# A gated attention and state-space kernel: skip term by a diagonal, tail tables in the lag stream, gates by a selection, and a refitted order

## The chip, the cores and the metric

One core of a Trainium2 chip runs the whole kernel. The metric is the device time of one execution in microseconds (us). The kernel before took a median of 389.49 us in three runs (388.06 to 393.62). One launch computes everything; inputs and output lie in DRAM.

The granted clock is the share of full speed that the profile reports. A run is called slow when it is more than 1.5% above the fastest of the same kernel in that series.

## The reference, cut to what matters

Two branches over the same 2048 x 512 input `x`, mixed by a gate per token:

```python
g = sigmoid((x * gate_w).sum(-1, keepdims=True))     # one gate per token
a = attention(x, wq, wk, wv, wo, beta)               # 32 heads, 4 segments of 512 tokens, with a memory
b = state_space(x, A, B, C, log_dt, Dskip)           # long convolution K * x, plus x * Dskip
return g * a + (1 - g) * b
```

The kernel computes the convolution as a transform over 4096 points cut in two: a first level, then 16 "lags" (pairs of frequencies), each with a product of spectra, then an output stage. In the profile the kernel falls into four stretches: until the last product that builds the table of powers ("tables end"); from there to the last exponential of the attention scores; the lags that remain until the last of them is stored to DRAM ("last V store"); and the end, with sixteen final DVE instructions and the output stores. Attention and lags share the engines wherever their order allows it.

The profiles name the engines so: PE is TensorE, which does the matmuls and leaves their results in PSUM; DVE is VectorE, ACT is ScalarE, POOL is GpSimd; SP is SyncE, whose queue issues the DMA transfers. An evacuation is a copy of results out of PSUM.

## The kernel before

Instructions are not issued in the order in which they are written. A small list scheduler in the kernel takes, for each engine, the ready operation with the lowest `key`; estimated costs decide when it is ready. The keys of attention, tables and lags come from eight tuned numbers. Which operation may hold a PSUM bank pair follows from the same order.

```python
KEYS = (11.26, 11.5, 60.5, 67.9, 3.16, 10.8, 43.9, 16.9)
PEN, MASKD = 6.53, 25
...
o.key = (self.key if key is None else key)
...
GA, TA0, TT0, TT = KEYS[:4]                  # attention group gi of (s, hg): key TA0 + GA * (8*s + 2*hg + gi)
tail(TT0 + 4 * TT + KEYS[6])                 # lag t: key k0 + 4 + KEYS[4] * t
```

The gates stand as one column per block of 128 tokens; the final stage needs them with 16 tokens a partition. They go through DRAM to change shape:

```python
if s == 3:
    S.dma(lambda: bass.AP(gbuf, 0, [[1, 128], [128, 16]]), lambda: ap(gcolT, n=16), 8192, r=gcolP, w=[dG], slow=True)
    S.dma(lambda: ap(g4T, n=16), lambda: bass.AP(gbuf, 0, [[16, 128], [1, 16]]), 8192, r=[dG], w=[g4T])
    op("DVE", 0.2, lambda e: e.tensor_scalar(ap(omg4T, n=16), ap(g4T, n=16), -1.0, 1.0, ALU.mult, ALU.add), ...)   # L899
```

The skip term `x * Dskip` is formed on DVE from a second load of `x`, and added to the result in PSUM by a product with the identity:

```python
for gq in range(4):
    S.dma(... xj <- x, 524288 ...)
    op("DVE", c_f1(2048), lambda e, u=u: e.tensor_tensor(u, u, dskbT (fp32, broadcast), ALU.mult), key=k0 + 45)    # L1266
    ...
    for bl in range(4):
        mm(e, ap(P, n=512), ap(ident, n=128), ap(u, bl * 512, n=512), True, False)
        for c in range(2):
            i = mm(e, ap(P, n=512), ap(G2T, c * 128, n=128), ap(V2, ...), False, c == 1)
        op("DVE", c_dps(512), ... e.scalar_tensor_tensor(aj, P, omg4T, aj, ALU.mult, ALU.add) ...)                  # L1281, the last sixteen
```

A lag reads its own slice of one table (`Dt`) and slices of two 1 MB tables (`M2`, `N1`) that are loaded once. The spectral product needs the negated imaginary part of K, which DVE makes for each lag.

The softmax here doesn't subtract the row's maximum and nothing guards it: scores larger than these inputs give would overflow.

## Time and profile before

| | before, first profile | before, profiled again |
|---|---|---|
| time, us | 398.8 | 386.63 |
| span, us; mean granted clock | 397.0; .886 | 384.8; .92 |
| tables end | 256.6 | 246.8 |
| last score exponential ends | 301.5 | 287.4 |
| last V store begins | 370.4 | 356.3 |
| first of the last sixteen DVE instructions | 380.8 | 367.0 |

The first profile is what I had for the prediction. The second was taken with the experiments. A line of stretches gives, after the span, the busy time of PE, weight loads, DVE, ACT and POOL, with the number of instructions, then the granted clock, the share of DMA and its GB/s. These are the four stretches of the second profile:

```profile
0.00:246.80 246.80, 216.72 (x2653) 98.99 (x2654) 215.42 (x419) 215.87 (x291) 3.15 (x9) 0.94 0.21 58
246.80:287.40 40.60, 29.81 (x506) 12.73 (x505) 26.00 (x57) 29.76 (x35) 0.00 (x0) 0.77 0.63 203
287.40:356.30 68.90, 67.53 (x414) 26.07 (x412) 58.14 (x87) 40.68 (x43) 0.00 (x0) 0.99 0.71 205
356.30:384.80 28.50, 13.87 (x52) 5.37 (x49) 10.99 (x16) 1.37 (x2) 0.00 (x0) 0.75 0.54 189
```

### The profile page before, as it was taken

To read this page: it belongs to the slowest core of one execution; us is meant where nothing else is said; L and a number is where in the kernel's file an instruction comes from. 1 tells how busy PE (TensorE), PEld (TensorE's weight loads), DVE (VectorE), ACT (ScalarE), POOL (GpSimd) and SP (SyncE) were. 2 spreads that over 40 slices of the span, in tenths; PEclk is the share of its full clock that TensorE was granted. 3 is DMA by queue.
4 is the path that set the end of the run, shared out by engine and by line. 5 is a ranking of instruction groups with operands and counts; after the bars stand their busy time and mean duration, and the time that the engine had idled before them with its cause. 6 is when DMAs were issued, how large, how long until landed. Compare 5 with 4: busy or idle time off the path is not lost.

```text
span 397.0 us, 8521 instructions
## 1 busy us (share of the span) xinstructions
PE 334.2 (84%) x3578; PEld 146.6 (37%) x3619; DVE 311.6 (78%) x579; ACT 288.6 (73%) x369; POOL 3.2 (1%) x9
## 2 busy tenths in 40 slices
PE   5876598899798799989999999919798999999283
PEld 3333143333344333534545434405234433333131
DVE  4889979977659887989898699827676899888164
ACT  4999979968768968968898999918775587555300
POOL 1000000000000000000000000000000000000000
PEclk9996579958769959999999999976958999999879
DMA  8910003000334430021000101123992967876573
GB/s 201 302 38 2 2 0 107 2 0 0 107 107 117 134 132 2 2 37 41 14 2 3 33 3 41 17 90 141 294 296 46 325 192 182 227 211 185 183 264 159
DMA packets 41238, 42.10 MB, mean 106 GB/s; under 512 B 18928, under 2 KB 34544, under 8 KB 40816
## 3 DMA queue, kind: packets, MB, share of 16 engines
q1 hardware_dynamic: 41200, 41.56, 35.4%
q8 instruction: 28, 0.46, 0.5%
q14 instruction: 10, 0.08, 0.1%
HBM read 28.30 MB, written 13.25 MB: 105 GB/s over the span
## 4 chain that ended last, share of the span: by engine, by line
PE 50%; DVE 22%; DMA 12%; ACT 10%; issue 3%; SPq 1%; DVEq 0%; ACTq 0%
PE psum L709 48%; ACT sb L1015 5%; DVE sb L257 4%; DMA sb<-in_A_x_dram 4%; DVE sb L1138 3%; DMA scr_gbuf<-sb 3%; DVE sb L1135 3%; DVE sb L1133 3%; ACT sb L256 2%; DVE sb L1281 2%; PE psum L1045 2%; DMA sb<-in_A_wq_dram 1%; DMA sb<-scr_V 1%; SPq L252 1%; DMA scr_abuf<-sb 1%
## 5 line engine op out<-in xcount | busy, mean ns | idle before, releaser
L709 PE MATMUL psum<-sb 128*32 128x20 bf16 (+12 forms) x3362 | 317.0, 283 | 50.2 <-DVE sb L1019 8.4
L709 PEld LDWEIGHTS psum<-sb 128*128 128x128 bf16 (+4 forms) x3403 | 131.0, 98 | 232.3 <-issue 106.2
L1015 ACT ACTIVATE sb<-psum 128x1024 bf16<-128x1024 f32 x160 | 156.8, 1027 | 31.6 <-PE psum L709 30.9
L256 ACT ACTIVATE sb<-psum 128x1024 bf16<-128x1024 f32 (+4 forms) x103 | 81.7, 808 | 42.3 <-PE psum L709 36.6
L257 DVE CAST sb<-psum 128x512 bf16<-128x512 f32 (+2 forms) x60 | 50.6, 845 | 32.2 <-PE psum L709 31.6
L1138 DVE TENSOR_TENSOR sb<-sb 128x512 bf16<-128x512 bf16 (+3 forms) x52 | 34.7, 667 | 1.4
L1133 DVE TENSOR_TENSOR sb<-sb 128x512 bf16<-128x512 bf16 (+3 forms) x52 | 34.6, 665 | 0.8
L1135 DVE TENSOR_TENSOR sb<-sb 128x512 bf16<-128x512 bf16 (+3 forms) x52 | 34.2, 657 | 0.0
L259 ACT ACTIVATE sb<-psum,sb 128x512 bf16<-128x512 f32 x30 | 20.7, 690 | 4.9 <-PE psum L709 3.5
L1281 DVE SCALAR_TENSOR_TENSOR sb<-psum,sb 128x512 bf16<-128x512 f32 x16 | 10.9, 745 | 12.6 <-DMA sb<-scr_abuf 12.5
L260 DVE TENSOR_SCALAR sb<-psum,sb 128x512 bf16<-128x512 f32 x18 | 13.4, 746 | 2.5 <-PE psum L709 1.8
L1045 PE MATMUL psum<-sb 128*128 128x128 bf16 x128 | 11.5, 242 | 0.8 <-ACT sb L259 0.5
L1019 DVE TENSOR_TENSOR sb<-sb 128x512 bf16<-128x512 bf16 (+1 forms) x21 | 10.3, 501 | 2.1 <-ACT sb L1015 2.1
L1235 DVE TENSOR_TENSOR sb<-sb 128x1024 bf16<-128x1024 bf16 x16 | 11.1, 693 | 0.6
L1239 DVE TENSOR_TENSOR sb<-sb 128x1024 bf16<-128x1024 bf16 x16 | 11.1, 692 | 0.6
L1053 DVE TENSOR_TENSOR sb<-psum,sb 128x512 bf16<-128x512 bf16 x16 | 11.1, 691 | 0.5
L256 ACT ACTIVATE sb<-sb 128x512 bf16<-128x512 f32 (+2 forms) x21 | 11.3, 578 | 0.3
L1237 DVE TENSOR_TENSOR sb<-sb 128x1024 bf16<-128x1024 bf16 x16 | 10.9, 684 | 0.0
L1045 PEld LDWEIGHTS psum<-sb 128*128 128x128 bf16 x128 | 9.0, 109 | 3.7 <-issue 1.3
L1072 DVE TENSOR_TENSOR sb<-psum,sb 128x256 bf16<-128x256 f32 x24 | 9.0, 418 | 0.4
L925 DVE TENSOR_SCALAR sb<-psum 128x512 bf16<-128x512 f32 x12 | 8.2, 686 | 1.3 <-ACT sb L924 1.2
L1266 DVE TENSOR_TENSOR sb<-sb 128x2048 bf16<-128x2048 bf16 x4 | 9.1, 2284 | 0.0
(64 smaller groups left out, 129.6 us busy)
## 6 DMA issues: line engine op xcount, KB each, us to landing
sb<-in_A_x_dram SPq DMA_DIRECT2D x12, 512.0 KB, 5.5
sb<-c_D SPq DMA_DIRECT2D x16, 320.0 KB, 7.0
scr_Z<-sb SPq DMA_DIRECT2D x16, 256.0 KB, 2.6
sb<-scr_Z SPq DMA_DIRECT2D x4, 1024.0 KB, 11.4
scr_V<-sb SPq DMA_DIRECT2D x16, 256.0 KB, 5.4
sb<-scr_V SPq DMA_DIRECT2D x16, 256.0 KB
scr_abuf<-sb SPq DMA_DIRECT2D x16, 128.0 KB, 3.0
sb<-scr_abuf SPq DMA_DIRECT2D x4, 512.0 KB, 5.5
```

What stands on the lines that cost most here:

```text
L256: fa = lambda e: e.activation(dst(), src(), ACT.Copy)
L257: fd = lambda e: e.tensor_copy(dst(), src())
L259: fa = lambda e: e.activation(dst(), src(), ACT.Copy, scale=scale())
L260: fd = lambda e: e.tensor_scalar(dst(), src(), scale(), None, ALU.mult)
L709: mm = lambda e, o_, l, r_, st, sp, **kw: e.matmul(o_, lhsT=l, rhs=r_, start=st, stop=sp, skip_group_check=True, **kw)
L1015: op("ACT", c_act(1024), lambda e, P=P, pT=pT, sj=sj: e.activation(ap(pT, sj * 1024, n=1024), ap(P, n=1024), ACT.Exp, scale=0.25), r=[P], ...
L1045: i = e.transpose(ap(P, tb * 256 + gi * 128, n=128), ap(ra[gi], tb * 128, n=128), ap(ident, n=128))
L1053: op("DVE", c_dps(512), lambda e: e.tensor_tensor(ap(o1, dims=[[128, 4], [16, 8], [1, 16]]), ap(P, dims=[[256, 4], [32, 8], [1, 16]]), ap( ...
L1133: op("DVE", c_tt(256 * n), lambda e: e.tensor_tensor(run(tile, ne, dst, 1), run(tile, ne, src, sstep), pwv(0), ALU.mult), r=rd + [pw], w=w ...
L1135: op("DVE", c_tt(256 * n), lambda e: e.tensor_tensor(run(t2, n, 0, 1), run(tile, ne, src, sstep), pwv(1), ALU.mult), r=rd + [pw], w=[t2])
L1138: op("DVE", c_tt(256 * n), lambda e: e.tensor_tensor(D_(), D_(), ap(t2, n * 128, [[-n * 128, 2], [2 * n, 64], [1, 2 * n]]), ALU.add), r=[t ...
L1281: op("DVE", c_dps(512), lambda e, P=P, aj=aj, bl=bl, b4=b4: e.scalar_tensor_tensor(ap(aj, bl * 512, n=512), ap(P, n=512), ap(omg4T, b4, n= ...
```

## The change

Its intent is to take work off DVE and off the DRAM path, and then to mix attention and lags anew. In five parts, as the prediction letters them:

- (a) The gates are laid out by a product with a 0/1 selection on PE instead of the trip through DRAM.
- (b) The skip term becomes four matmuls of 128 columns with a diagonal of `Dskip`, for which `x` transposed is kept on chip. The load of `x` and DVE's four products go.
- (c) The two big tables become slices of the lag's own table. The sign moves into a subtraction, so the negation of K goes.
- (d) The relu of K may run on ACT; two more attention groups are masked on DVE (`MASKD`).
- (e) New keys, single shifts of keys (`ORDER`) and new cost estimates, so another order of everything.

A filler that would keep PE busy in its waits is in the code too, but `FILL = 0` leaves it out: PE stays idle in its waits. The core of the diff, cut:

```diff
-PEN = 6.53
-MASKD = 25
-KEYS = (11.26, 11.5, 60.5, 67.9, 3.16, 10.8, 43.9, 16.9)
+FILL, FILL0, FILLM = 0, 15.0, 0.1
+PEN = 4.0
+MASKD = 23
+KEYS = (12, 2.52, 50.32, 60, 5.74, 12.49, 34.52, 14.72)
+ORDER = {'proj2.1': -6.4, 'oph3.2': 4.1, 'oph2.3': -11.9, 'grp1.3.0': -9.7, 'oph1.3': 2.3, 'K6': 2.9, 'grp2.2.0': -23.2}
...
-        o.key = (self.key if key is None else key)
+        o.key = (self.key if key is None else key) + ORDER.get(self.tag, 0.0)
...
-    S.dma(lambda: bass.AP(gbuf, 0, [[1, 128], [128, 16]]), lambda: ap(gcolT, n=16), 8192, r=gcolP, w=[dG], slow=True)
-    S.dma(lambda: ap(g4T, n=16), lambda: bass.AP(gbuf, 0, [[16, 128], [1, 16]]), 8192, r=[dG], w=[g4T])
+    op("DVE", 0.3, ... gselT = gcolT (broadcast) * selT, 128 elements ...)
+    op("PE", 0.3, lambda e: mm(e, ap(P4, n=16), ap(gselT, n=128), ap(selT, 8, n=16), True, True), ...)
...
-    op("DVE", c_dps(512), ... rk = max(P, 0) ...)
+    op("ANY", 0.0, None, r=[P], w=[rk], alts={"ACT": ... ACT.Relu ..., "DVE": ... max ...})
...
-    S.dma(lambda: ap(M2, n=4096), lambda: hm2[:], 1048576, w=[M2])
-    S.dma(lambda: ap(N1, n=4096), lambda: hn1[:], 1048576, w=[N1], key=k0 + 1.5)
-    S.dma(lambda Dt=Dt: ap(Dt, n=1280), lambda t=t: hD[t], 327680, w=[Dt], key=S.key - 8)
+    S.dma(lambda Dt=Dt: ap(Dt, n=1792), lambda t=t: hD[t], 458752, w=[Dt], key=S.key - 8)
-    op("DVE", c_ts4(512), ... K3[512:] = -K3[1024:] ...)
-    op("DVE", c_tt(1024), ... Y = Y + Tt ...)
+    for co in range(2):
+        op("DVE", c_tt(512), ... Y[co] = Y[co] (ALU.add if co else ALU.subtract) Tt[co] ...)
...
-    S.dma(... xj <- x, 524288 ...)
-    op("DVE", c_f1(2048), ... u = u * dskbT ...)
-    mm(e, ap(P, n=512), ap(ident, n=128), ap(u, bl * 512, n=512), True, False)
+    for k in range(4):
+        i = mm(e, ap(P, k * 128, n=128), ap(xTT, k * 2048 + b4, [[16, 128]]), ap(diagT, k * 128, n=128), k == 0, False)
```

## The prediction

> **What bounds the kernel now.** I read the page first, then the chain of waits, then busy time in stretches, then the time order of instructions around the two holes that those showed, and last the groups by shape. The profiled execution took 398.8 us by its own time and is marked slow, against a median of 389.49 (388.06 to 393.62); I use its stretches for differences, not for the level.
>
> ```profile
> PE 334.2 (84%) x3578; PEld 146.6 (37%) x3619; DVE 311.6 (78%) x579; ACT 288.6 (73%) x369; POOL 3.2 (1%) x9
> ```
>
> No engine is full over the span, so the sums alone cannot set the time. The stretches (table fill until the last table product; rest of the attention groups; the lags that remain; the end) show who is short where. Columns after the span: busy time of PE, weight loads, DVE, ACT, POOL, granted clock, DMA share, GB/s.
>
> ```profile
> 0.00:256.10 256.10, 222.94 (x2620) 101.63 (x2650) 215.89 (x418) 216.16 (x290) 3.16 (x9) 0.89 0.21 56
> 256.10:305.70 49.60, 36.38 (x553) 16.07 (x554) 28.52 (x61) 32.23 (x39) 0.00 (x0) 0.72 0.53 170
> 305.70:370.44 64.74, 62.26 (x363) 23.84 (x371) 56.35 (x84) 38.89 (x41) 0.00 (x0) 1.00 0.75 217
> 370.44:397.00 26.56, 12.62 (x51) 5.08 (x50) 10.86 (x16) 1.29 (x2) 0.00 (x0) 0.84 0.55 199
> ```
>
> So: 256 us in which ACT and DVE are both 84% busy; 50 us in which nobody is above 73%; 65 us in which PE is at 96% while ACT has 40% free; 27 us of end. The second stretch holds a hole in which everything stands still:
>
> ```profile
> 256.00:260.00 4.00, 1.77 (x19) 0.84 (x17) 0.50 (x2) 3.59 (x5) 0.00 (x0) 1.00 0.02 4
> 260.00:264.00 4.00, 0.00 (x0) 0.00 (x0) 0.00 (x0) 0.00 (x0) 0.00 (x0) 0.77 0.01 2
> 264.00:268.00 4.00, 1.43 (x38) 0.53 (x38) 2.53 (x8) 0.00 (x0) 0.00 (x0) 0.50 0.67 227
> 268.00:272.00 4.00, 4.00 (x156) 2.49 (x154) 2.85 (x6) 3.49 (x4) 0.00 (x0) 0.50 0.73 303
> 272.00:276.00 4.00, 4.00 (x142) 2.42 (x126) 3.76 (x11) 2.99 (x4) 0.00 (x0) 0.52 0.02 4
> ```
>
> Its cause, in the chain and in the waits: the gates' trip through DRAM. L899 is the 16-element subtraction that needs them.
>
> ```profile
> 252.34 11.52 DMA scr_gbuf<-sb
> 263.88 1.50 DMA sb<-scr_gbuf
> ...
> DVE sb L899 <- DMA sb<-scr_gbuf: 8.9, 1, 8.9
> PE psum L709 <- DVE sb L1019: 8.4, 2, 8.2
> ```
>
> At the end the chain runs through two transfers and then the sixteen last DVE products:
>
> ```profile
> 370.44 3.36 DMA scr_V<-sb
> ...
> 373.82 4.94 DMA sb<-scr_V
> ...
> 378.80 2.75 PE psum L709 x6
> ```
>
> ```profile
> 380.79 10.92 DVE L1281 SCALAR_TENSOR_TENSOR sb<-psum,sb 128x512 bf16<-128x512 f32 x16 [12.55 <-DMA sb<-scr_abuf]
> ```
>
> DVE starts those only when the attention rows are back (380.79, two us after V), and then runs without a gap. The end is DVE's and the transfers', not PE's.
>
> [...]one tiny instruction of the gates held all DVE for 8.87 us. [...]80 to 88 us shows 0.50 with PE fully busy[...]. [...]The gates' store is 2,048 pieces of 4 bytes: 8 KB took 11.5 us, where 128 KB of attention rows took 3.0. [...]The skip products (bf16 by fp32) measure 2284, four of them.
>
> **The change part by part.** Counts are from the two programs' instruction orders, durations from the groups of before.
>
> (a) Gates by a selection. Two transfers and the hole go; a 128-element fp32 DVE product comes (0.3 us, an estimate between the 0.19 of 32 and the 0.44 of 272 elements) with one 16-column fp32 matmul (under 0.5 us, an estimate; a one-column bf16 one reads 0.16). The holes were DVE 8.87, PE 8.22, ACT 8.57 at the same time, so all of it is on the path: minus 8. The half clock after it lasts about 10 us with PE busy; at full clock half of that, but DVE is nearly full there too, so I count 2 more. Minus 10.
>
> (b) The skip term. Gone: four x loads (2 MB), four products of 2.28 = 9.1 us DVE, 16 identity matmuls of 512 columns. New: 64 matmuls of 128 columns, so the same columns; one diagonal product of 0.69. Eight of the sixteen blocks' skip matmuls can be done while V is under way[...], but the end was DVE's: nothing there on the path. What counts is DVE in the lag stage.
>
> (c) Tail tables inside the lag stream. The two 1 MB loads at 264 us become 128 KB more on each of 16 lag loads: the same bytes. The negation of K goes: 16 x 0.286 = 4.6. The sum is split into a subtraction and an addition: 16 x (2 x 0.42 - 0.68) = 2.6 more.
>
> (d) Re-balance. Relu of K: 12 x 0.686 = 8.2 leave DVE, 7.3 come to ACT. Two more groups are masked on DVE: 4 x 0.41 + 2 x 0.68 = 3.0 more there, and 4096 columns less on PE[...]. Evacuations: seven of 1024 move from ACT (-7.2) to DVE (+8.6); three fewer scaled ones on DVE (-2.2), the small ones cancel.
>
> DVE: -9.1 - 4.6 + 2.6 - 8.2 + 3.0 + 8.6 - 2.2 + 1.0 for the diagonal and the selection = -8.9, 303 left. ACT +1 (290).[...] As sums: little.
>
> (e) Order, the largest part. Before, only 3 of 64 PE steps of the lags stand ahead of the last attention score; after, 38. Before, one lag costs PE (64.7 - 5.2 for six output steps - 2)/15.3 = 3.75 us. What stands behind the last score then falls from 64.7 to 26/64 x 60 + 5 = 29 us: minus 35. It is not free: the evacuations and products of those lags go among the groups. Adding the orders' instructions up to the last score, ACT's busy time there grows from 249 to 268 and DVE's from 250 to 273. Before, 305.7 - 8.9 = 297 us held them at 84%. At the same density they need 319 to 325, say 322. So 322 + 29 + 26.6 = 378 against 397: minus 19, with (a)'s stall in it.
>
> A second way, by DVE: its work up to the last table product falls by 8% (masks and skip products gone or later, relus on ACT), so that point moves from 256.1 to about 235. Behind it DVE's work up to the last lag product grows from 90 to 101 in summed durations. Before it took 368.3 - 256.1 - 8.9 = 103 us, 87%; now 112 to 116. 235 + 114 + the unchanged 28.7 to the end = 378. The two agree: minus 19.
>
> **The rivals.** First: the lags among the groups fight for the PSUM pairs of the scores and for ACT, so density falls, to 81% say: 333 + 29 + 27 = 389, minus 8, about 381. Against it: in the last lag stretch ACT has 40% free and in the groups PE has. For it: ACT and DVE lack only 16% from 0 to 256 us. Second: everything is simply DVE's sum, so minus 9, and the hole's 9 us were slack that DVE catches up: about 380. Against it: in the hole ACT and PE stood too. Third: the groups with lags between pack better, 88%: 307 + 29 + 27 = 363, minus 34, about 356. For it: the tuned order numbers and step costs were fitted anew; PE, ACT and DVE now have work of two kinds at once. Fourth: clock. [...]a few us either way. A fifth, no gain at the end: I expect it, as the attention rows' load still goes out last.
>
> **Range and chances.** 389.5 - 19 = 370.5; I lean a little to the third rival, as an order is seldom kept that does not pack better: 369. Range 356 to 381, from the third rival to the first and second. Faster than 381.7 needs only (a) to hold nearly whole, which is the surest part: 0.86. Within 2%: 0.12. Slower: 0.02, only if order and clock go wrong together.
>
> **What would show it.** (a) No stretch of 4 us without work between the third and last quarter; the 16-element product waits under 1 us. (b) No DVE products of 2.28 us; sixteen last products still back to back, about 11 us; from the last V store to the end still 25 to 27. (c) No negation in the lags. (e) Last score exponential about 310 to 325 us and 26 to 32 us from there to the last V store; ACT over 80% busy up to it; DVE still fullest, about 303. Wrong would be: a last score past 335 (the first rival), a wait on the lag loads in place of the two big ones, or a mean clock well under 0.88.

Cut from it, where marked, is what no trace or run of this case shows: general rules on the order of engines, on the clock and on rates, the number of PSUM banks, the reason given for the fourth rival, and two times of PE: that of the 4096 columns in (d), and PE's sum. PE's sum was set beside those of DVE and ACT and did not go into the forecast, whose own sum is whole: it came to minus 19 (378 against 397), so 389.5 - 19 = 370.5, and 369 with the lean to the third rival. The 2 us for the clock in (a) are the author's estimate, from about 10 us at a granted clock of .50.

## More of the kernel before

Executions of one kernel differ by some per cent here, and the longer ones show a lower granted clock of TensorE: the kernel before took from 383.79 us at a mean of .94 to 400.71 us at .883.

The four skip products are one group in the page of the first profile, with the mean of one in ns behind the sum:

```profile
L1266 DVE TENSOR_TENSOR sb<-sb 128x2048 bf16<-128x2048 bf16 x4 | 9.1, 2284 | 0.0
```

They run one at a time, with products of the lags between them. The first began at 312.2 us; the other three in the time order of DVE (start, duration, engine, line):

```profile
321.13 2.29 DVE L1266 TENSOR_TENSOR sb<-sb 128x2048 bf16<-128x2048 bf16 x1
325.71 2.29 DVE L1266 TENSOR_TENSOR sb<-sb 128x2048 bf16<-128x2048 bf16 x1
330.17 2.28 DVE L1266 TENSOR_TENSOR sb<-sb 128x2048 bf16<-128x2048 bf16 x1
```

## The result, and the profile after

The kernel after took a median of 375.25 us (374.76 to 376.67, four runs, all fast, clocks .932 to .938) beside 390.26 us for the kernel before (388.06 to 393.62, four runs). The ratio of the fast runs is 0.961, with a 95% interval from 0.954 to 0.969: faster. A ratio here is the mean time of one kernel's fast runs over the mean of the other's fast runs of the same rounds, so not quite the ratio of the two medians. Forecast were 369 us, 20.5 less than the 389.49 known then; measured are 15.0 less.

In a later series (chip 15) the same kernel took 375.72, 376.23 and 379.61 us in its fast runs and 382.8 to 385.4 in its slow ones; the ratio there is 0.973 (0.962 to 0.984). So its size differs from series to series, its sign does not.

The busy line of the page, and the four stretches of the first profile of the kernel after, columns as above:

```profile
PE 320.2 (85%) x3610; PEld 144.1 (38%) x3649; DVE 302.1 (81%) x578; ACT 289.0 (77%) x374; POOL 3.2 (1%) x9
```

```profile
0.00:230.50 230.50, 195.12 (x2395) 88.72 (x2419) 198.12 (x379) 199.50 (x270) 3.17 (x9) 0.92 0.21 61
230.50:315.10 84.60, 78.83 (x905) 34.04 (x916) 68.24 (x135) 66.62 (x81) 0.00 (x0) 0.98 0.59 182
315.10:348.50 33.40, 32.65 (x219) 13.21 (x221) 25.07 (x50) 21.58 (x25) 0.00 (x0) 1.00 0.52 152
348.50:374.90 26.40, 13.56 (x98) 8.13 (x98) 10.62 (x16) 1.28 (x2) 0.00 (x0) 0.81 0.59 207
```

And the same of the later profile:

```profile
0.00:231.00 231.00, 199.87 (x2417) 89.30 (x2419) 197.86 (x379) 199.58 (x270) 3.17 (x9) 0.92 0.22 61
231.00:314.30 83.30, 79.15 (x916) 33.60 (x916) 68.22 (x135) 66.60 (x81) 0.00 (x0) 1.00 0.61 185
314.30:347.70 33.40, 32.97 (x223) 13.18 (x221) 25.08 (x50) 21.58 (x25) 0.00 (x0) 1.00 0.55 157
347.70:374.40 26.70, 14.43 (x100) 8.33 (x98) 10.81 (x16) 1.29 (x2) 0.00 (x0) 0.84 0.55 197
```

The two agree to 1.3 us in every stretch. Side by side, with the mark of the last score placed at the end of its exponential in all profiles:

| stretch, us | before (slow, .886) | before again (.92) | forecast | after | after again |
|---|---|---|---|---|---|
| until tables end | 256.6 | 246.8 | 235 | 230.5 | 231.0 |
| to the last score | 44.9 | 40.6 | 87 | 84.6 | 83.3 |
| to the last V store | 68.9 | 68.9 | 29 | 33.4 | 33.4 |
| end | 26.6 | 28.5 | 27 | 26.4 | 26.7 |
| span | 397.0 | 384.8 | 378 | 374.9 | 374.4 |

The forecast column is the prediction's own sum before it took the difference to 397 from the measured 389.5. The picture is as forecast: 35 us leave the lag stretch, 40 to 43 us come among the attention groups, and the tables end earlier. But compared between profiles at a good clock, 384.8 (.92) against 374.4 (.938), the gain is 10.4 us. The timed gain is larger, since the runs of before in the first series (388 to 394 us) all took longer than the 386.63 of that profile.

At the end, the chain of waits and the time order of DVE (columns as above; in brackets how long it stood idle and what released it) show the same picture as before:

```profile
349.98 5.15 DMA scr_abuf<-sb
355.15 4.20 DMA sb<-scr_abuf
```

```profile
359.37 10.62 DVE L1312 SCALAR_TENSOR_TENSOR sb<-psum,sb 128x512 bf16<-128x512 f32 x16 [13.08 <-DMA sb<-scr_abuf]
```

Sixteen final instructions follow one another without a gap, after 13.08 us of waiting for the attention rows. No wait stands ahead of the subtraction of the gates, and no DVE instruction of 2.28 us is left.

### The profile page after: what moved, and what is told of

Same layout as the page of the kernel before. It is cut to its first block, busy times and chain, and to the rows that moved or that the text cites. A ratio compares the mean times of both kernels' runs of the same rounds, so it can differ in the third digit from the quotient of the medians.

```text
span 374.9 us, 8574 instructions
## 1 busy us (share of the span) xinstructions
PE 320.2 (85%) x3610; PEld 144.1 (38%) x3649; DVE 302.1 (81%) x578; ACT 289.0 (77%) x374; POOL 3.2 (1%) x9
## 4 chain that ended last, share of the span: by engine, by line
PE 55%; DVE 23%; ACT 11%; issue 4%; DMA 4%; SPq 1%; DVEq 0%
PE psum L738 54%; ACT sb L1048 6%; DVE sb L260 4%; DVE sb L1171 3%; DVE sb L1168 3%; DVE sb L1312 3%; DVE sb L1166 2%; ACT sb L259 2%; DMA sb<-in_A_wq_dram 1%; DVE sb L847 1%; PE psum L1078 1%; DMA scr_abuf<-sb 1%; DVE sb L846 1%; SPq L255 1%; DMA sb<-scr_abuf 1%
## 5 line engine op out<-in xcount | busy, mean ns | idle before, releaser
L738 PE MATMUL psum<-sb 128*32 128x20 bf16 (+14 forms) x3394 | 305.0, 274 | 42.7 <-ACT sb L1048 12.7
L738 PEld LDWEIGHTS psum<-sb 128*32 128x32 bf16 (+4 forms) x3433 | 129.5, 97 | 215.0 <-issue 85.9
L1048 ACT ACTIVATE sb<-psum 128x1024 bf16<-128x1024 f32 x160 | 157.0, 1027 | 20.0 <-PE psum L738 19.0
L259 ACT ACTIVATE sb<-psum 128x512 bf16<-128x512 f32 (+4 forms) x97 | 75.8, 794 | 35.2 <-PE psum L738 29.6
L260 DVE CAST sb<-psum 128x512 bf16<-128x512 f32 (+2 forms) x66 | 57.5, 881 | 25.6 <-PE psum L738 25.1
L1052 DVE TENSOR_TENSOR sb<-sb 128x512 bf16<-128x512 bf16 (+1 forms) x27 | 13.4, 507 | 2.2 <-ACT sb L1048 2.0
L1270 DVE TENSOR_TENSOR sb<-sb 128x512 bf16<-128x512 bf16 x32 | 13.6, 424 | 1.0
L1263 DVE TENSOR_TENSOR sb<-sb 128x1024 bf16<-128x1024 bf16 x16 | 11.0, 686 | 4.0 <-ACT sb L259 4.0
L263 DVE TENSOR_SCALAR sb<-psum,sb 128x512 bf16<-128x512 f32 x15 | 11.2, 745 | 1.3 <-PE psum L738 0.7
L259 ACT ACTIVATE sb<-sb 128x512 bf16<-128x512 f32 (+2 forms) x17 | 9.8, 600 | 2.5 <-PE psum L738 2.5
L1086 DVE TENSOR_TENSOR sb<-psum,sb 128x512 bf16<-128x512 bf16 x16 | 11.1, 691 | 0.5
L1265 DVE TENSOR_TENSOR sb<-sb 128x1024 bf16<-128x1024 bf16 x16 | 11.0, 684 | 0.0
L1008 ACT ACTIVATE sb<-sb 128x512 bf16<-128x512 bf16 x12 | 7.6, 631 | 0.8 <-PE psum L738 0.7
L957 ACT ACTIVATE sb<-psum 128x512 bf16<-128x512 f32 x12 | 7.2, 597 | 0.4
```

Of the source, the lines that this page charges most:

```text
L259: fa = lambda e: e.activation(dst(), src(), ACT.Copy)
L260: fd = lambda e: e.tensor_copy(dst(), src())
L738: mm = lambda e, o_, l, r_, st, sp, **kw: e.matmul(o_, lhsT=l, rhs=r_, start=st, stop=sp, skip_group_check=True, **kw)
L1048: op("ACT", c_act(1024), lambda e, P=P, pT=pT, sj=sj: e.activation(ap(pT, sj * 1024, n=1024), ap(P, n=1024), ACT.Exp, scale=0.25), r=[P], ...
L1052: op("DVE", c_tt(d[0][1] * d[1][1] * d[2][1]), lambda e, pT=pT, d=d: e.tensor_tensor(ap(pT, dims=d), ap(pT, dims=d), ap(mask01, dims=[[0, ...
L1270: op("DVE", c_tt(512), lambda e, Y=Y, Tt=Tt, co=co: e.tensor_tensor(ap(Y, co * 512, n=512), ap(Y, co * 512, n=512), ap(Tt, co * 512, n=512 ...
```

## The experiments

Two theories stood against each other. The first is the prediction's: the hole of the gates is worth nearly its full length, and the new order is worth what it takes behind the last score less what it costs among the groups. The rival: the hole is slack that is caught up, and the gain is in DVE's sum or in the order alone. Most variants were scheduled afresh by the kernel's own scheduler, so one edit moves other operations too; the last series therefore has three runs in which the order of every engine is held, instruction for instruction, and only the part in question is put in or taken out.

**gates_only.** The kernel before with the selection of part (a), and nothing else.

```diff
 # kernel before
-    S.dma(... gbuf <- gcolT ...); S.dma(... g4T <- gbuf ...)
+    gselT = gcolT * selT on DVE; mm(P4, gselT, selT[8:]) on PE; omg4T = 1 - P4
```

> The kernel before with the gates re-laid by the selection and nothing else (4 of 64 lag steps ahead of the last group's last step, as before 3). Theory of the prediction: the hole of 8.2 to 8.9 us was on the path of all three engines, so 8 to 10 us faster than before, about 381, ratio 0.975 to 0.98. Rival (slack): DVE and ACT catch up in the half-idle stretch behind the hole, so under 3 us, ratio above 0.992.

Measured: 382.69 to 387.58 us (median 384.16, clocks .919 to .932), against 383.79 to 387.74 of the fast runs of the kernel before in that series. Ratio 0.996 (0.988 to 1.005): inside the 2%, its interval across 1. Its stretches were 248.5, 34.9, 70.7 and 28.2. Against the second profile of before, the stretch with the hole lost 5.7 us, and tables and lags gained 3.5 of them back. The selection alone, in a fresh schedule of the old keys, pays little that the time could show.

**gates_dram.** The kernel after with the gates through DRAM again, scheduled afresh.

```diff
 # kernel after
-    gselT = gcolT * selT; mm(P4, gselT, selT[8:]); omg4T = 1 - P4
+    S.dma(... gbuf <- gcolT ...); S.dma(... g4T <- gbuf ...); omg4T = 1 - g4T
```

> The changed kernel with the gates sent through DRAM again, all else kept (38 of 64 lag steps ahead, as changed). Theory of the prediction: the hole comes back whole, 8 to 10 us slower than the changed kernel, about 384, ratio to before 0.98 to 0.985. Rival (slack): the lags give the engines other work[...]: 377 to 379.

Measured: fast runs 382.5, 383.3 and 386.69 us, slow ones 388.44 and 399.07; ratio 1.000 (0.989 to 1.011). That figure comes out when the 388.44 is counted as fast and the 382.5 left out; the three fast runs alone (mean 384.2) against the 386.1 of the kernel before in the same rounds give 0.995. Either way nearly the whole gain is gone. Its profile, which fell in a slow run, shows DVE waiting 7.2 us for the gates. So part (a) looks needed for the gain, although alone it gives hardly any; but this is a fresh schedule.

**old_order.** All new operations with the old keys, costs and no shifts (`MASKD` stays 23): three of 64 lag steps of PE stand ahead of the last score, as before.

```diff
 # kernel after
-KEYS = (12, 2.52, 50.32, 60, 5.74, 12.49, 34.52, 14.72);  PEN = 4.0;  ORDER = {...}
+KEYS = (11.26, 11.5, 60.5, 67.9, 3.16, 10.8, 43.9, 16.9); PEN = 6.53; ORDER = {}
-    return k * (0.0025 + n / 2370.0)
+    return k * (0.014 + n / 2300.0)          # and the other step costs of before
```

> The changed kernel with the old order numbers and step costs (3 of 64 lag steps ahead of the last group's last step): the structure without the new order. Theory of the prediction: order is worth about 9 to 10 of the gain, so about 384 to 385; gates and DVE savings alone remain. Rival (order is nothing, the structure is all): 375 to 377. Second rival (order is nearly all): 388 and more.

Measured: fast runs 381.96, 384.96 and 386.49 us; ratio 0.996 (0.986 to 1.006). The stretch behind the last score was 69.8 us long. Hole, skip products and negation gone give almost nothing while the lags stay in one block behind the scores.

**new_order.** The kernel before with the new keys, shifts and costs; gates through DRAM, skip term by products, tables in one piece. 36 of 64 lag steps stand ahead of the last score.

```diff
 # kernel before
-KEYS = (11.26, 11.5, 60.5, 67.9, 3.16, 10.8, 43.9, 16.9)
+KEYS = (12, 2.52, 50.32, 60, 5.74, 12.49, 34.52, 14.72);  PEN = 4.0;  ORDER = {...};  step costs of after
```

> The kernel before with the new order numbers and step costs and nothing else (36 of 64 lag steps ahead). Theory of the prediction: 9 to 10 us faster than before, about 380, its hole at the gates still there. Rival (the order pays only with the tail tables inside the lag stream and with the DVE work taken off): within 4 us of before, since the two 1 MB loads and the skip products stand among the groups then.

Measured: 401.29 to 404.92 us in its fast runs; ratio 1.043 (1.033 to 1.052). On the old operations the order makes the kernel 4% slower. In its profile (clock .918) the stretches are 233.7, 90.1, 44.2 and 31.8, against 231.0, 83.3, 33.4 and 26.7 of the kernel after. No wait for the gates is in it. What is in it, in the time order of DVE, is this block, with the products of the last three lags queued behind it:

```profile
346.97 8.88 DVE L1267 TENSOR_TENSOR sb<-sb 128x2048 bf16<-128x2048 bf16 x4
```

The four skip products stand in the lag stretch, which is 10.8 us longer than that of the kernel after; the end is 5.1 longer too. That pointed at part (b), which I had held to be off the path.

**after_again.** The kernel after, unchanged, on chip 15, as a base for the next ones.

> The changed kernel once more, on the chip of the runs beside it, as their reference. All theories: 373 to 377 as on record; ratio to before 0.96 to 0.975, as before spreads from 384 to 395 with its granted clock while the changed kernel held within 2 us.

Measured: as told above, 375.72 to 379.61 us in the fast runs, ratio 0.973. With its slow runs it spread over 9.7 us, so it does not hold within 2 us as expected.

**new_order_gates.** new_order with the selection of part (a).

```diff
 # new_order
-    S.dma(... gbuf <- gcolT ...); S.dma(... g4T <- gbuf ...)
+    selection on PE as in the kernel after
```

> The kernel before with the new order and the selection for the gates; the four skip products, the x loads, the two 1 MB loads and the negation stay. Theory now (parts need each other): the hole's 8 to 10 us come off the 403 of the new order alone, so 392 to 395, still slower than before, because the four skip products of 2.28 us stand in one block ahead of the last lag products on DVE. Rival (the gates were the whole of it): within 3 us of the changed kernel, 375 to 378.

Measured: fast runs 401.11 to 405.83 us; ratio 1.039 (1.029 to 1.048). Against new_order's 1.043 this is no difference, and not the 8 to 10 us expected. In this schedule the trip of the gates cost nothing that the time shows; and what makes the order bad on the old operations is not the gates.

**skip_load.** The kernel after with part (b) undone: second load of `x`, four products, identity matmuls. Scheduled afresh.

```diff
 # kernel after
+    S.dma(... xj <- x, 524288 ...)
+    op("DVE", c_f1(2048), ... u = u * dskbT ..., key=k0 + 45)
-    for k in range(4): mm(P[k], xTT[k], diagT[k])
+    mm(P, ident, u[bl])
```

> The changed kernel with its skip term undone: x loaded again, four fp32 products on DVE, identity matmuls. Theory now: the four products (9.1 us) stand together between the last lag products and the last sixteen, the x loads only open when the attention buffers are free, so 7 to 12 us slower than the changed kernel, 382 to 387. Theory of the prediction (skip term off the path at the end): within 3 us of the changed kernel.

Measured: fast runs 393.56 to 399.38 us; ratio 1.021 (1.007 to 1.036), about 19 us above the fast runs of after_again. The four products are one block again, ahead of the last lag products:

```profile
349.88 8.89 DVE L1299 TENSOR_TENSOR sb<-sb 128x2048 bf16<-128x2048 bf16 x4
```

But the loss is not where that block is: in its profile the lag stretch grew by 3.9 us, tables by 10.4 and the stretch to the last score by 5.7. A fresh schedule moved other things, and the clock was lower as well (.893 to .908 in its fast runs, .926 to .938 in those of after_again); which of the two did it is not shown. The run shows that undoing (b) costs much, not that the products themselves cost it. For that the order has to be held.

**before_again.** The kernel before once more, for a profile at a better clock.

> The kernel before, for a profile in its fast state. If the hole is as in the slow profile: 8 to 9 us with DVE, PE and ACT all idle at the gates, table products ending 5 to 8 us earlier than the 256.6 of the slow profile. Rival: the hole is shorter than 5 us in a fast execution, and the gates' small worth alone (2 us) is explained by that.

Measured: 386.63 us (one run, so its state is unknown; clock .92). Its hole:

```profile
254.97 0.17 DVE L899 TENSOR_SCALAR sb<-sb 128x16 f32<-128x16 f32 x1 [8.21 <-DMA sb<-scr_gbuf]
```

So the hole is as long as in the slow profile, and the rival of a short one is out. The tables ended 9.8 us earlier, more than the 5 to 8 expected.

The next three hold the order of PE, DVE and ACT.

**hole_out.** The kernel before without the two transfers of the gates, in the same order of instructions. The subtraction reads the gates in their wrong layout, so the result is wrong (relative error 0.039); the work is the same.

```diff
 # kernel before, after scheduling: order kept
-    two DMA operations of the gates
-    omg4T = 1 - g4T
+    omg4T = 1 - gcolT
```

> The kernel before with its order held instruction for instruction on PE, DVE and ACT; only the two gate transfers are taken out of the queue and the 16-element subtraction reads the gates in the wrong layout (a wrong result on purpose). Theory now (the hole is mostly given back in the old order, because the lag stage behind it starts from the tables' transfers and is full on PE): 2 to 4 us faster than before. Theory of the prediction (all 8 us on the path): 8 to 10 us faster.

Measured: fast runs 378.95 and 384.19 us, slow ones to 388.21, beside 389.36 to 393.61 of the kernel before; ratio 0.975 (0.938 to 1.011), so unclear by time. The stretches of the profile are clearer. This is the one that held the hole:

```profile
253.10:284.10 31.00, 25.74 (x508) 11.42 (x505) 26.11 (x56) 29.16 (x35) 0.00 (x0) 1.00 0.81 265
```

It took 31.0 us instead of 40.6, with the same work in it and a clock of 1.00 instead of .77. The lag stretch behind it is 0.4 us longer and the end 1.3: nothing big is given back. (The trip also made the queue of SP wait, in the first profile 11.2 us for the store of the gates, and the loads of the two big tables were issued right behind it, at 253.79 and 254.26 us in before_again. With the trip out, the DMA share of the stretch was .81 instead of .63.) So in its own order the hole is worth 9.6 us: its 8.2 and 1.4 more. That the 1.4 are the clock's is an estimate; no run parts the two. The tables stretch took 6.3 us more than in before_again at the same order and a clock of .91 instead of .94. I do not count that for the edit: the gates were ready for their store only some 4 us before that stretch ended (at 242.5 of 246.8 us in before_again; issued at 252.3 of 256.6 in the first profile). It shows how much two executions differ: their whole spans, at the same mean clock of .92, are only 1.6 us apart.

**hole_in.** The kernel after with the trip added: the gates are stored and loaded again, and one more 16-element subtraction, ten DVE instructions later, waits for them.

```diff
 # kernel after, after scheduling: order kept
+    dma gbuf <- gcolT;  dma betaT <- gbuf
+    op("DVE") omg4T = 1 - betaT          # ten DVE instructions on
```

> The changed kernel with its order held; the gates' two transfers put back into the queue beside the selection, and one more 16-element DVE subtraction, ten DVE instructions on, that waits for them. Theory now (in the new order PE, ACT and DVE are full behind the gates, nothing takes up a hole): 7 to 10 us slower than the changed kernel, about 384. Rival (given back as in the old order): 2 to 4 us slower.

Measured: fast runs 393.71, 398.54 and 398.73 us, about 20 above the fast runs of after_again; ratio to before 1.014 (0.993 to 1.036). The kernel before was itself some 4 us slower in this series than in that of after_again, so by the two ratios it is nearer 16. Its profile, in a slow run, shows the wait on DVE, then one 4 us slice in the midst of it, then the whole stretch to the last score:

```profile
279.44 0.17 DVE L1394 TENSOR_SCALAR sb<-sb 128x16 f32<-128x16 f32 x1 [17.16 <-DMA sb<-scr_gbuf]
```

```profile
272.00:276.00 4.00, 0.00 (x0) 0.00 (x0) 0.00 (x0) 0.00 (x0) 0.00 (x0) 0.50 0.00 0
235.90:338.60 102.70, 82.20 (x916) 34.36 (x916) 68.34 (x136) 66.90 (x81) 0.00 (x0) 0.90 0.51 150
```

An instruction of 0.17 us stopped all engines, and the stretch grew from 83.3 to 102.7 us. That is more than in the kernel before, since the store of the gates now stands in the queue of SP behind four loads of K (scr_K; 8.4 us from issue to landing in the median, and in the first profile of the kernel after their issue holds the queue for 9.10 us): it was issued at 266.6, 4.3 us after DVE had run dry at 262.3, and took another 11.2 to land. The last three stretches together grew by 19.1, so next to nothing of it was caught up.

**products_in.** The kernel after with eight fp32 products of 1024 elements on DVE, put ahead of lag 13's products: the elements of the four skip products, where new_order had them.

```diff
 # kernel after, after scheduling: order kept
+    8 x op("DVE") accT[:1024] = xTT[:1024] * gmaskT (fp32)     # ahead of the first product of lag 13
```

> The changed kernel with its order held and eight fp32 DVE products of 1024 elements (about 1.2 us each, in sum as much as the four skip products) put in ahead of the lag product of lag 13, where the skip products stood when they were brought back; they write to a dead buffer, so the result stays right. Theory now (the skip products lie on the path at the end of the lags): 8 to 10 us slower than the changed kernel. Rival (DVE has room there, 5 of 10 us were idle from 340 to 350; the 16 us of the undone skip term were order and clock): under 4 us.

Measured: fast runs 385.36, 386.7 and 387.06 us at a clock of .931: 386.4 in the mean against 377.2 of after_again, so 9.2 more. By the two ratios to before, 0.987 (0.973 to 1.001) and 0.973, it would be 5.5; I go by the profiles, which have like clocks (.931 and .938). The block in the time order of DVE, and its lag stretch:

```profile
337.39 10.02 DVE L1389 TENSOR_TENSOR sb<-sb 128x1024 bf16<-128x1024 bf16 x8
```

```profile
314.90:358.80 43.90, 34.42 (x223) 13.59 (x221) 34.78 (x58) 21.56 (x25) 0.00 (x0) 0.92 0.41 120
```

10.02 us of DVE made the lag stretch 10.5 us longer (43.9 against 33.4); the other stretches are the same within 0.4 us. Here, in one block, a microsecond of DVE is a microsecond of the kernel.

**no_nudges.** The kernel after without the seven single shifts.

```diff
 # kernel after
-ORDER = {'proj2.1': -6.4, ...}
+ORDER = {}
```

> The changed kernel without the seven hand-set offsets of order (all other numbers kept; no instruction differs, only their order). Theory that the new order's worth is its coarse shape (lags among the groups): within 3 us of the changed kernel. Rival (the order is tuned to one instruction list, and any perturbation costs): 5 to 10 us slower, which would then also be in the runs that undid the gates or the skip term with a fresh schedule.

Measured: fast runs 381.74 and 385.92 us, slow ones 387.64 to 391.51; ratio 0.980 (0.948 to 1.013). Its fast mean is 6.6 us above that of after_again; by the two ratios it is 3. Two fast runs and four slow ones do not settle it, but 3 to 7 us is the size that a fresh schedule may move the time by without any operation changed, and so the doubt in all runs that were scheduled afresh.

Put together, with each ratio to the kernel before of its own series:

| | old keys | new keys |
|---|---|---|
| old operations | 1 | 1.043 |
| old operations, gates by selection | 0.996 | 1.039 |
| new operations | 0.996 | 0.961 and 0.973 |
| new operations, gates through DRAM | not run | 1.000 (0.995, see gates_dram) |
| new operations, skip term by products | not run | 1.021 |

## Why the prediction was right or wrong

The direction and the range held: 375.25 lies between 356 and 381. The point was 6 us too low. By its steps:

**(a), the gates: right where the order is held.** Forecast were 8 us of hole and 2 of clock. With the order held, taking the hole out shortened its stretch by 9.6, with the clock there back at 1.00. Putting one into the kernel after cost 19.4 in the stretch. The second rival, a hole that DVE catches up, fell with these two. That the fresh schedule of gates_only kept only part is told by its own stretches; by time its gain is within the spread of before, where 8 to 10 us were expected.

**(b), the skip term: wrong in one clause.** "Nothing there on the path" fits the end (in the first profile of after 32 of the 64 skip matmuls ran ahead of PE's wait of 6.37 us for V), which went from 28.5 to 26.7 us at most (in skip_load it took 29.9, so even there it is not certain). "What counts is DVE in the lag stage" pointed the right way, but the 9.1 us went only into DVE's sum, diluted over a stage. In the new order the scheduler makes the products one block in the lag stretch, where DVE is 75% busy (25.08 of 33.4 us) and yet the next lags can't go on without it. There such a block costs its full length (products_in: 10.5 for 10.02). In these runs (b) paid only with (e), and (e) only with (b): the prediction added the parts up, and the table above shows that they do not add. Two limits: of the runs behind this only products_in held the order, and none tried (b) by itself with the old keys. And a rival is untested: in the kernel before the four products stood one at a time between the lags; spread like that in the new order they may cost less than the block.

**(c), (d): right as sums, not isolated.** DVE is at 302.1 us, forecast 303; ACT at 289.0, forecast 290. The split sum reads 32 x 0.424 = 13.6 us against 11.1 before, 2.5 more, forecast 2.6. The waits of PE hold none on a lag table at all, in either profile of after. No run took the tables or the negation back by themselves.

**(e), the order: mechanism right, one term mis-sized.** The stretch behind the last score fell by 35.5 us, forecast 35. The table shows it at 33.4 where 29 was forecast, because the prediction's mark of 305.70 lay 4.2 us behind the end of the last exponential, on both sides of the difference (with the mark moved, its 87 us to the last score are 83, and 83.3 to 84.6 were measured). The tables ended at 231, forecast 235. The last exponential ended at 314 to 315, inside the forecast "about 310 to 325". What failed is the sentence "At the same density they need 319 to 325, say 322", together with the level it was set against: its density of 84% came from a slow profile. In the profile at the better clock, up to the last score and without the 8.2 us of hole, 287.4 - 8.2 = 279.2 us, ACT is (215.87 + 29.76)/279.2 = 88% busy and DVE (215.42 + 26.00)/279.2 = 86.5%. After, up to 314.3, both are at 84.7%: (199.58 + 66.60) and (197.86 + 68.22). Density did fall, and as far as the first rival had it: by 3.3 points for ACT and 1.8 for DVE, where it had 3 (81% from 84). Its minus 8 is nearer to the 10.4 between the two spans than the forecast of 19. At 88% ACT's 266.2 us would have fitted into 303, and at 86.5% DVE's 266.1 into 308. So 7 to 12 us of the expected gain went there; the forecast of 19 and the 10.4 of the two spans differ by 8.6.

The forecasts of the stretches themselves came within 5 us each; it is the tables stretch of the kernel before that was 10 us shorter at the better clock.

Where the density went can be read from ACT's waits up to the last score (waited for: sum, times, longest). The kernel before, profiled again; its 7.9 is the hole:

```profile
ACT sb L1015 <- PE psum L709: 18.5, 19, 7.9
ACT sb L256 <- PE psum L709: 9.6, 16, 1.6
```

The kernel after, profiled again; L1048 is the score exponential, L259 an evacuation of PSUM:

```profile
ACT sb L259 <- PE psum L738: 19.8, 26, 3.3
ACT sb L1048 <- PE psum L738: 18.7, 31, 2.1
```

Without the hole ACT waited 20.2 us for PE before and 38.5 after. And PE had no room: its busy time up to the last score rose from 216.72 + 29.81 = 246.5 to 199.87 + 79.15 = 279.0. That is 88.3% of 279.2 and 88.8% of 314.3. From the tables' end to the last score alone PE is busy 79.15 of 83.3 us, 95%, at full clock, with ACT at 80% and DVE at 82%; in the kernel before, from the end of the hole (255.0), it was 28.56 of 32.4 us, 88%, at a clock of .76. The prediction counted what ACT and DVE would gain among the groups, 19 and 23 us, and left out what PE would, 32.5; against its first rival it even said that PE has time free there. With PE at its own density the last score comes at 279.0/0.883 = 316, against 314.3 measured; since the 279.0 was measured afterwards, this is a check and no forecast. This term is read from traces, not shown by a run: none took PE's work alone away from the groups. The rival's own cause, a fight for the PSUM pairs of the scores, is not excluded: PE's waits for the score exponentials, which free those pairs, grew from 8.3 to 12.4 us.

The other rivals: the third, better packing, did not come, and the lean towards it was wrong. The fourth, a lower clock, did not show (mean .932 to .938). The fifth was right: the attention rows' load is still what the last sixteen wait for.

Left open: why skip_load lost twice what the products cost; how the 6.8 us that new_order takes more in the stretch to the last score, and the 5.1 at its end, divide among its operations; and the tail tables by themselves.

## What to carry to other kernels

An operation off today's path is not free in tomorrow's order: four products that stood singly beside a long PE stretch, and whose removal with the rest of (a) to (d) showed no clear gain in the old order, became one block in the new one, and a block of their length there cost its full 10 us. So try parts that remove work together with an order that uses the room; runs with the order held tell their shares apart. When work is moved into a busy stretch, add up every engine there, PE too, and take each at its own density from a profile in the same state as the times that it will be compared with. And look for tiny instructions that wait for a transfer through DRAM: in hole_in one of 0.17 us left DVE idle for 17.16 us, and from 268 to 276 us no engine was busy.

## What else the traces show

- The granted clock. In 4 us slices of hole_in it was 1.00 from 240 to 268 us, .52 from 268 to 272 and .50 from there to 284, where the slices end. In hole_out, the kernel before without its hole, it was 1.00 from the tables' end to the last score, and in before_again, with the hole, .77. But the same program, with PE busy in both executions, ran at about half clock in one and at full clock in the other, in the same 16 us. The first profile of before as stretches, then its 512-column matmuls there (count, busy us, mean ns):

```profile
76.00:84.00 8.00, 7.50 (x53) 2.95 (x54) 6.25 (x9) 5.31 (x7) 0.00 (x0) 0.62 0.01 2
84.00:92.00 8.00, 7.78 (x46) 2.83 (x46) 6.27 (x10) 5.66 (x7) 0.00 (x0) 0.53 0.00 0
```

```profile
L709 PE MATMUL psum<-sb 128*128 128x512 bf16 x10 | 4.5, 612 | 0.4 <-ACT sb L1015 0.2 <-issue 0.2
```

The second profile of before, the same two views:

```profile
76.00:84.00 8.00, 7.20 (x80) 2.86 (x80) 7.77 (x12) 7.09 (x10) 0.00 (x0) 1.00 0.01 2
84.00:92.00 8.00, 7.98 (x68) 3.14 (x68) 7.86 (x17) 7.79 (x12) 0.48 (x1) 1.00 0.00 0
```

```profile
L709 PE MATMUL psum<-sb 128*128 128x512 bf16 x20 | 5.0, 380 | 0.0
```

  A mean of 612 ns against 380: the matmuls really were slower, by a factor of 1.6. From 80 to 88 us PE was busy without a break (8.00 of 8 us) at .50. What set the clock there is not shown; nor does any run tell how much of this kernel's spread, 383.79 us at .94 to 400.71 at .883 or 4.4%, comes from such stretches.
- The store of the gates, 2,048 pieces of 4 bytes. Its 8 KB took 11.5 us to land in the kernel before and 11.2 in hole_in, several times the 1.8 us of 128 KB of attention rows in the median of the kernel after.
- The selection that turns a column per block into rows on PE instead. In the first profile of after it is one DVE product of 128 fp32 elements, 0.29 us, a matmul of 16 columns (two records of 0.25 us in the mean, 0.3 us busy in sum), and a subtraction of 0.17 us with no wait ahead of it.
